# Attention and two MLPs on one core: the float64 sign kept by a parametric ReLU, the rounding given to the engine that is free, another order of the first sixteen steps, reloads in place

## The chip, the cores and the metric

The kernel runs on one core of a Trainium2 chip. The metric is the device time of one execution in microseconds, of which the median over several executions is compared. An execution that is recorded by the hardware profiler gives the trace; its span runs from its first to its last instruction.

## The reference

Attention over q, k, v (4 batches, 8 heads, 576 rows, 64 wide) is the sum of a coarse part, softmax over rows averaged by four, repeated four times, and a local part, softmax over the rows at a distance under four. Its output, 2304 rows of 512, goes through two layers of the same form:

```python
def _moe_ref(x, w_in, w_out):          # layer 1; _moe2_ref is the same with its own weights
    h = x @ w_in                       # 2304x512 @ 512x2048
    r = np.maximum(h, 0.0)
    g = r * r
    return (g @ w_out).astype(np.float32)   # 2304x2048 @ 2048x512
```

q, k and v are float32. The weights w_in and w_out are float64.

## The kernel before

**Tiles and steps.** The 2304 rows are cut into nine tiles of 256 rows, the 2048 hidden columns into eight pieces p of 256. A step (n, p) multiplies tile n with piece p of w_in (`mm_h`, L883: 24 matmuls, two halves of 12), takes ReLU and square on ScalarE (L895, L897), splits g into a high part (L907, ScalarE) and a low part (L934, VectorE), and multiplies with piece p of w_out (`mm_y`, L967: 24 matmuls). Every operand is split in two because TensorE takes fp32r: `xH`, `xL` of a tile (`split_x`, L390 and L858), high and low halves of a weight. The product y of a step stands in TensorE's order after the h of the next step. n from 0 to 8 is layer 1, n from 9 to 17 layer 2, where w_out is multiplied in seven products instead of eight (`mm_y2`, L950). The first sixteen steps belong to tiles 0 and 1 together; `LEAD` says how far tile 0 is ahead. Both tiles need each weight only once it has been converted.

**Weights of layer 1** (`convert1`, sixteen pieces of 1 MB float64). A piece lands in a buffer `s` as pairs of 32-bit words. ScalarE scales the upper words to a float32 in `gp` (1024 columns) or `ga` (two of 512) (L693), ScalarE shifts the lower words (L695), VectorE puts the sign bit of the upper word into the lower one (L697), VectorE joins the two (L702), ScalarE rounds the result to the high part (`evac`, L390), VectorE or GpSimd subtracts it to get the low part (L713). There are two such sets of buffers, so two pieces are in work at a time. `convert2` does the same for layer 2 in 32 halves during layer 1 (L739, L741, L743, L747) and stores the joined float32 in DRAM (`ws`). `reload` fetches it back when tile 8 has used a piece for the last time: into a buffer `ld`, of which there are two, then high part (L390) and low part (L829). `quarters` prepares the seven products' sums of w_out.

**Attention.** Rows of a batch are taken in five groups of 116. Per batch, `load_qk` transposes q and k in five chunks (L450, evacuated by L390, pooled by four on VectorE at L457), `heads_of` does the coarse part, `group` the local one: scores (L586), maximum, exponential, sum, division (L619, on VectorE or GpSimd), transposition (L623), product with the values (L641, values loaded by `values`, L556), addition into the tile `xr` (L653). Tile 0 needs groups 0 to 2 of batch 0, tile 1 needs groups 2 to 4.

**What sets the order.** All instructions of an engine run in the order in which the program issues them. That order is worked out by `Order`, a list scheduler with a cost for every operation: each thread has a priority, a number from the tables `CP, CD, GP, UP, QP, VP, HP`, and asks for an engine and a time. An operation that may run on several engines gives a list, and the engine is taken on which it would end first. `dvp` and `pool` stand for VectorE and GpSimd with a common port in that planner, `dve` and `fast` for VectorE without it. Until the first step TensorE is given small products without use (`fill`, L1121) in every gap of the plan. All DMAs are issued by SyncE, in order; each waits for the DMA eight before it.

## Time and profile before

| | us |
|---|---|
| three executions, median | 926.19 (924.8 to 1109.7) |
| the profiled execution | 928.45 |
| its span | 926.6 |
| TensorE busy with matmuls | 895.9 (97%) |
| VectorE busy | 533.5 (58%) |
| ScalarE busy | 525.2 (57%) |
| GpSimd busy | 70.4 (8%) |

A share over the span says little here, since the first 92 us (attention of batch 0, weights on their way) and the rest are different stages. One reads first where TensorE is idle or slow, and then what it waits for there.

### The profile page before, as it was taken

Reading aid. Unit: us, or ns where it says so; the run is one execution under the profiler, and the core shown is the slowest. Engines: PE = TensorE matmul, PEld = TensorE weight load, DVE = VectorE, ACT = ScalarE, POOL = GpSimd, SP = SyncE. Lnnn points to the kernel's source line nnn. Section 1 sums busy time; section 2 is a strip of 40 time slices with the busy share of each in tenths; the row PEclk is TensorE's granted clock in tenths of the full one; section 3 lists DMA queues with packets and bytes.
Section 4 is the critical chain, followed back from the end, with each engine's and each line's share of the span. In section 5 each row is a group of like instructions: output and inputs, shape, how many; then the busy total and the mean of one; then the engine's idle time right before and its main releaser. Section 6 shows DMA issues by size and latency. Waiting matters only on the chain.

```text
span 926.6 us, 20891 instructions
## 1 busy us (share of the span) xinstructions
PE 895.9 (97%) x8712; PEld 860.9 (93%) x8712; DVE 533.5 (58%) x1072; ACT 525.2 (57%) x1029; POOL 70.4 (8%) x72
## 2 busy tenths in 40 slices
PE   8967999999999999999999999999999999999996
PEld 5566999999989999999999999999999999999996
DVE  5898875375685656554412466646556464545454
ACT  4787884466467566664535665455555554545443
POOL 4102210020030100000100001000000000000000
PEclk9978999999999999999999999999999999999999
DMA  9997931135255665753203441101010010100000
GB/s 173 248 247 187 229 100 36 48 109 125 52 163 170 185 196 183 238 182 102 93 1 138 137 159 48 46 1 46 2 46 24 24 47 1 47 1 24 1 24 23
DMA packets 91998, 90.48 MB, mean 98 GB/s; under 512 B 62208, under 2 KB 67840, under 8 KB 91904
## 3 DMA queue, kind: packets, MB, share of 16 engines
q1 hardware_dynamic: 91904, 89.15, 33.9%
q8 instruction: 68, 1.11, 0.5%
q14 instruction: 26, 0.21, 0.1%
HBM read 70.25 MB, written 18.87 MB: 96 GB/s over the span
## 4 chain that ended last, share of the span: by engine, by line
PE 85%; DVE 5%; DMA 4%; ACT 3%; SPq 2%; issue 1%; ACTq 0%; DVEq 0%
PE h L883 40%; PE y L967 19%; PE at L950 12%; PE y L950 4%; PE at L967 2%; DMA s<-in_moe_w_out_dram 1%; PE at L450 1%; DVE S L930 1%; DMA ld<-in_v_dram 1%; SPq L437 1%; DVE ld L1072 1%; PE at L641 1%; PE at L586 1%; PE at L516 1%; PE at L476 1%
## 5 line engine op out<-in xcount | busy, mean ns | idle before, releaser
L883 PE MATMUL h<-xH,w 128*128 128x256 f32 x2304 | 318.7, 281 | 0.0
L883 PEld LDWEIGHTS h<-xH,w 128*128 128x128 f32 x2304 | 289.0, 189 | 2.4 <-issue 1.6
L895 ACT ACTIVATE h<-h 128x512 f32<-128x512 f32 x144 | 83.9, 583 | 195.6 <-PE h L883 195.5
L967 PE MATMUL y<-g,w 128*128 128x256 f32 x1536 | 193.1, 280 | 0.2 <-ACT g L907 0.2
L967 PEld LDWEIGHTS y<-g,w 128*128 128x128 f32 x1536 | 182.2, 189 | 3.2 <-issue 1.2
L883 PE MATMUL h<-xL,w 128*128 128x256 f32 x1152 | 180.2, 279 | 0.0
L934 DVE TENSOR_TENSOR g<-h,g 128x512 fp32r<-128x512 f32 x144 | 98.6, 684 | 106.2 <-ACT g L907 105.8
L883 PEld LDWEIGHTS h<-xL,w 128*128 128x128 f32 x1152 | 154.7, 189 | 0.0
L930 DVE TENSOR_TENSOR S<-h,S 128x128 f32<-128x128 f32 x144 | 41.9, 291 | 154.8 <-ACT g L907 150.5
L913 ACT CAST SH<-S 128x512 fp32r<-128x512 f32 x72 | 44.7, 621 | 93.2 <-DVE S L930 91.0
L897 ACT ACTIVATE h<-h 128x512 f32<-128x512 f32 x144 | 84.2, 585 | 3.1
L907 ACT CAST g<-h 128x512 fp32r<-128x512 f32 x144 | 84.8, 589 | 1.5
L939 DVE TENSOR_TENSOR gSL<-S,SH 128x512 fp32r<-128x512 f32 x72 | 51.1, 709 | 9.9 <-ACT SH L913 1.5
L858 POOL TENSOR_TENSOR xL<-xr,xH 128x512 fp32r<-128x512 f32 x12 | 18.0, 1504 | 408.2 <-ACT xH L390 408.2
L950 PE MATMUL at<-w,SH 128*128 128x256 f32 x224 | 45.0, 282 | 1.4 <-ACT SH L913 1.4
L930 DVE TENSOR_TENSOR S<-S,h 128x128 f32<-128x128 f32 x144 | 41.2, 286 | 5.0
L950 PEld LDWEIGHTS at<-w,SH 128*128 128x128 f32 x224 | 34.0, 188 | 2.3 <-ACT SH L913 2.2
L950 PE MATMUL at<-w,g 128*128 128x256 f32 x240 | 34.6, 279 | 0.4 <-DVE g L934 0.4
L950 PE MATMUL at<-w,gSL 128*128 128x256 f32 x112 | 32.1, 287 | 1.9 <-DVE gSL L939 1.9
L950 PEld LDWEIGHTS at<-w,g 128*128 128x128 f32 x240 | 30.8, 188 | 0.6 <-DVE g L934 0.6
L950 PE MATMUL y<-w,g 128*128 128x256 f32 x192 | 27.6, 279 | 0.0
L457 DVE TENSOR_REDUCE qkd<-at 128x256 f32<-128x1024 f32 (+1 forms) x19 | 20.7, 1106 | 9.3 <-ACT qkT L390 9.1
(252 smaller groups left out, 1238.0 us busy)
## 6 DMA issues: line engine op xcount, KB each, us to landing
ld<-ws SPq DMA_DIRECT2D x24, 512.0 KB, 3.2
s<-in_moe_w_in_dram SPq DMA_DIRECT2D x32, 256.0 KB, 3.7
s<-in_moe_w_out_dram SPq DMA_DIRECT2D x16, 512.0 KB, 10.9
ws<-ga SPq DMA_DIRECT2D x32, 256.0 KB, 2.4
ld<-in_moe_w_in_dram SPq DMA_DIRECT2D x11, 512.0 KB
ld<-in_moe_w_out_dram SPq DMA_DIRECT2D x11, 512.0 KB, 4.7
xr<-ys SPq DMA_DIRECT2D x9, 512.0 KB, 3.7
vw<-in_v_dram SPq DMA_DIRECT2D x68, 64.0 KB, 3.0
```

The costliest lines, as they stand in the source:

```text
L457: nc.vector.tensor_reduce(out=qkd[:, :, :, 32 * c:32 * c + n // 4], in_=got.rearrange("p z m (g r) -> p z m g r", r=4), op=ALU.add, axis=AX.X,
L858: engine().tensor_tensor(out=xL[n % NXL][:, ks], in0=xr[i][:, ks], in1=xH[n % NXL][:, ks].bitcast(F32), op=ALU.subtract)
L883: nc.tensor.matmul(out=o, lhsT=wt[p, 0][:, 1084:1340][:, fs] if w is wL and kk == 0 and p in ODD else w[:, kk, fs], rhs=x[:, kk], start=(i ...
L895: nc.scalar.activation(out=h, in_=h, func=AF.Relu)
L897: nc.scalar.activation(out=h, in_=h, func=AF.Square)
L907: nc.scalar.copy(g_of(i, 0), h)
L913: nc.scalar.copy(late2["SH"], late2["S"])
L930: nc.vector.tensor_tensor(out=dst, in0=a, in1=b, op=op)
L934: nc.vector.tensor_tensor(out=g_of(i, 1), in0=h, in1=g_of(i, 0).bitcast(F32), op=ALU.subtract)
L939: nc.vector.tensor_tensor(out=late2["SL"], in0=late2["S"], in1=late2["SH"].bitcast(F32), op=ALU.subtract)
L950: nc.tensor.matmul(out=seven(n, m - 1), lhsT=lhsT, rhs=quarter(p, w, low), start=p == 0 and x == 0 and m not in (2, 3, 6), stop=p == NP - ...
L967: nc.tensor.matmul(out=yb[e // 2][:, (e % 2) * 256:(e % 2) * 256 + 256], lhsT=w[:, fi, e * 128:e * 128 + 128], rhs=g[:, fi * 256:fi * 256 ...
```

## The change

It has five parts. (1) L693 and L739 scale the upper word with a parametric ReLU (slope 2^32 for negative values) in place of a plain copy, so that the sign survives the shift; L697 and L743, which carried it over on VectorE, are gone (16 instructions of 1024 columns, 32 of 512). (2) The rounding to the high part in `convert1` goes to ScalarE or VectorE, whichever the planner finds free first; the cost of `fast` has no port in it. (3) The first sixteen steps follow the string `TURNS`, digit by digit the tile: three of tile 0, two of tile 1, and so on; before they were three of tile 0, then tile 1 and tile 0 in turn until tile 0 had its eight. (4) The numbers that set priorities are others, and three are new. (5) `reload` loads straight into the place of the low part, rounds from there and subtracts in place, and takes no buffer `ld`; `quarters` runs as one thread in place of two.

```diff
-LEAD = 2
+TURNS = "0001101011000111"
-CP, CD, GP, UP = -0.47, 0.09, -1.99, -1.02
-QP, VP, HP = -0.59, 0.34, -0.14
+CP, CD, GP, UP = -0.705, 0.436, -1.416, -0.816
+QP, VP, HP = -0.053, 0.649, 0.159
+CK, H1, G1 = 0.243, 0.689, -0.199
...
         for g, c, n in parts:
             yield act(n)
-            nc.scalar.activation(out=g, in_=wf[:, c:c + n], func=AF.Copy, scale=2.0 ** -112)
+            nc.scalar.activation(out=g, in_=wf[:, c:c + n], func=AF.Prelu, scale=2.0 ** -112, alpha=2.0 ** 32)
         yield act(1024)
         nc.scalar.activation(out=wl, in_=wl, func=AF.Copy, scale=2.0 ** -29 - 2.0 ** -49, bias=-0.5)
-        yield dvp(1024)
-        nc.vector.scalar_tensor_tensor(
-            out=w32[:, :, 0], in0=w32[:, :, 1], scalar=-2 ** 31, in1=w32[:, :, 0], op0=ALU.bitwise_and, op1=ALU.bitwise_or
-        )
...
         for g, c, n in parts:
-            yield act(n)
-            evac(hi[:, c:c + n], g)
+            yield [act(n), fast(n)]
+            if o.eng == "ACT":
+                evac(hi[:, c:c + n], g)
+            else:
+                nc.vector.tensor_copy(hi[:, c:c + n], g)
...
-        n = yield from f_ld.take()
-        t = ld[n].bitcast(F32)
-        yield dma(128 * 4096)
-        nc.sync.dma_start(out=t, in_=wscr[p][kind])
         hi = weight(p, kind, 0, 2).rearrange("p k f -> p (k f)")
-        yield act(1024)
-        evac(hi, t)
-        for lo, c, n1 in pieces(p, kind, 1, 2, 0, 1024):
+        some = pieces(p, kind, 1, 2, 0, 1024)
+        for lo, c, n1 in some:
+            yield dma(128 * 4 * n1, 4096 if n1 == 1024 else 2048)
+            nc.sync.dma_start(out=lo.bitcast(F32), in_=wscr[p][kind][:, c:c + n1])
+        for lo, c, n1 in some:
+            yield act(n1)
+            evac(hi[:, c:c + n1], lo.bitcast(F32))
+        for lo, c, n1 in some:
             tt = yield either(n1)
-            engine().tensor_tensor(out=lo, in0=t[:, c:c + n1], in1=hi[:, c:c + n1].bitcast(F32), op=ALU.subtract)
-        f_ld.put(n, tt)
+            engine().tensor_tensor(out=lo, in0=lo.bitcast(F32), in1=hi[:, c:c + n1].bitcast(F32), op=ALU.subtract)
...
-    steps = []
-    for p in range(NP + LEAD):
-        steps += [(0, p)] * (p < NP) + [(1, p - LEAD)] * (p >= LEAD)
+    steps = [(int(n), TURNS[:i].count(n)) for i, n in enumerate(TURNS)]
...
-    o.lane(2, [(98, quarters(0)), (98, quarters(1))])
+    o.lane(1, [(98, quarters())])
```

Since the planner works on these numbers, most rows of the first stage stand elsewhere; line numbers of the changed kernel are two or three off. Three places follow. `s_88`, `s_89`, `s_90` are the float64 pieces of w_in for p = 0, 1, 2; `s_65`, `s_68`, `s_71` those of w_out; `w_629`, `w_715`, `w_663` (before) and `w_499`, `w_680`, `w_576` (after) the converted p = 0 and 1 of w_in and p = 0 of w_out; `e_84` holds the scores of groups 2 to 4 and `e_95` their values.

VectorE before, up to the division of group 4 (`e_84<-e_84,nmb_76`), for which TensorE waits at 58.8 us:

```order
L702 SCALAR_TENSOR_TENSOR gp<-gp,s_89 128x1024
L613 TENSOR_REDUCE nmb_76<-e_84 128x8
L615 TENSOR_SCALAR nmb_76<-nmb_76 128x8
L697 SCALAR_TENSOR_TENSOR s_68<-s_68 128x1024
L713 TENSOR_TENSOR w_715<-gp,w_715 128x1024
L653 TENSOR_TENSOR xr_104<-y,outd 128x4x58
L702 SCALAR_TENSOR_TENSOR ga_86<-ga_86,s_68 128x512
L653 TENSOR_TENSOR xr_104<-y,outd 128x4x58
L702 SCALAR_TENSOR_TENSOR ga_87<-ga_87,s_68 128x512
L617 RECIPROCAL nmb_76<-nmb_76 128x8
L619 TENSOR_TENSOR e_84<-e_84,nmb_76 128x2x4x64
L697 SCALAR_TENSOR_TENSOR s_90<-s_90 128x1024
```

VectorE after, the twelve rows up to the same division:

```order
L655 TENSOR_TENSOR xr_103<-at_118,outd 128x4x24
L701 SCALAR_TENSOR_TENSOR gp<-gp,s_89 128x1024
L655 TENSOR_TENSOR xr_104<-at_118,outd 128x4x34
L711 CAST w_680<-gp 128x1024
L655 TENSOR_TENSOR xr_104<-at_118,outd 128x4x58
L607 TENSOR_TENSOR e_84<-at_117,nmb_76 128x2x4x64
L615 TENSOR_REDUCE nmb_76<-e_84 128x8
L617 TENSOR_SCALAR nmb_76<-nmb_76 128x8
L619 RECIPROCAL nmb_76<-nmb_76 128x8
L857 TENSOR_TENSOR xL_101<-xr_103,xH_99 128x512
L701 SCALAR_TENSOR_TENSOR ga_86<-ga_86,s_68 128x512
L621 TENSOR_TENSOR e_84<-e_84,nmb_76 128x2x4x64
```

Ahead of the division the sign instructions (L697) and the subtractions for `w_663` and `w_715` are gone from VectorE, a cast to `w_680` has come in, and the two additions of group 3 into `xr_104` stand behind it.

TensorE before, around the first step (`w_629`):

```order
L641 MATMUL y<-e_84,e_95 64x58 x16
L883 MATMUL h_120<-xH_99,w_629 128x256 x8
L883 MATMUL h_120<-xL_101,w_629 128x256 x4
L623 MATMUL at_118<-ident,e_84 128x128 x4
L883 MATMUL h_120<-xH_99,w_629 128x256 x8
L883 MATMUL h_120<-xL_101,w_629 128x256 x4
L883 MATMUL h_121<-xH_99,w_715 128x256 x8
L883 MATMUL h_121<-xL_101,w_715 128x256 x4
L641 MATMUL at_117<-e_84,e_95 64x58 x4
L641 MATMUL at_117<-e_84,e_95 64x54 x4
L641 MATMUL at_117<-e_84,e_95 64x58 x4
L641 MATMUL at_117<-e_84,e_95 64x54 x4
```

TensorE after, around the same step (`w_499`):

```order
L880 MATMUL h_120<-xH_99,w_499 128x256 x8
L880 MATMUL h_120<-xL_101,w_499 128x256 x4
L643 MATMUL at_118<-e_84,e_95 64x58 x16
L625 MATMUL at_117<-ident,e_84 128x128 x4
L880 MATMUL h_120<-xH_99,w_499 128x256 x8
L880 MATMUL h_120<-xL_101,w_499 128x256 x4
L880 MATMUL h_121<-xH_99,w_680 128x256 x8
L880 MATMUL h_121<-xL_101,w_680 128x256 x4
L643 MATMUL at_118<-e_84,e_95 64x58 x4
L643 MATMUL at_118<-e_84,e_95 64x54 x4
L643 MATMUL at_118<-e_84,e_95 64x58 x4
L643 MATMUL at_118<-e_84,e_95 64x54 x4
```

Group 3's product with the values, which stood ahead of the first step, stands between its two halves.

SyncE before, the loads that follow the values of groups 0 and 1 (`vw_108`, `vw_109`):

```order
L678 DMA s_88<-in_moe_w_in_dram 64x2x256 x4
L683 DMA s_65<-in_moe_w_out_dram 128x512 x2
L678 DMA s_89<-in_moe_w_in_dram 64x2x256 x4
L683 DMA s_68<-in_moe_w_out_dram 128x512 x2
L556 DMA e_95<-in_v_dram 64x4x64 x5
L678 DMA s_90<-in_moe_w_in_dram 64x2x256 x4
L556 DMA e_95<-in_v_dram 64x4x64 x4
L683 DMA s_71<-in_moe_w_out_dram 128x512 x2
L556 DMA e_95<-in_v_dram 64x4x64 x2
L678 DMA s_91<-in_moe_w_in_dram 64x2x256 x4
L556 DMA e_95<-in_v_dram 64x4x64
```

SyncE after, the loads that follow the values of group 0:

```order
L680 DMA s_88<-in_moe_w_in_dram 64x2x256 x4
L685 DMA s_65<-in_moe_w_out_dram 128x512 x2
L558 DMA vw_109<-in_v_dram 64x4x64 x4
L680 DMA s_89<-in_moe_w_in_dram 64x2x256 x4
L685 DMA s_68<-in_moe_w_out_dram 128x512 x2
L558 DMA e_95<-in_v_dram 64x4x64 x4
L680 DMA s_90<-in_moe_w_in_dram 64x2x256 x4
L558 DMA e_95<-in_v_dram 64x4x64
L685 DMA s_71<-in_moe_w_out_dram 128x512 x2
L558 DMA e_95<-in_v_dram 64x4x64 x3
L680 DMA s_91<-in_moe_w_in_dram 64x2x256 x4
L558 DMA e_95<-in_v_dram 64x4x64 x4
```

The weights for p = 0 go ahead of group 1's values; of the four loads for group 3 (the second four of `e_95`) three stand behind `s_71`, and group 4's four behind `s_91`.

## Rows read from the trace of the kernel before

**Rows 1.** The page: busy time of each engine, share of the span, instructions.

```profile
PE 895.9 (97%) x8712; PEld 860.9 (93%) x8712; DVE 533.5 (58%) x1072; ACT 525.2 (57%) x1029; POOL 70.4 (8%) x72
```

**Rows 2.** Stages: busy us (instructions) of each engine, granted clock, DMA share, GB/s.

```profile
25.00:49.80 24.80, 21.52 (x317) 13.00 (x316) 21.25 (x45) 19.35 (x42) 1.23 (x2) 0.98 0.98 244
49.80:91.70 41.90, 28.69 (x258) 27.14 (x255) 36.53 (x48) 32.22 (x45) 5.71 (x5) 0.81 0.93 217
91.70:538.00 446.30, 445.46 (x4703) 432.54 (x4700) 247.82 (x445) 264.72 (x530) 38.66 (x32) 1.00 0.45 133
538.00:594.00 56.00, 53.31 (x455) 52.06 (x454) 37.72 (x80) 33.75 (x63) 3.69 (x2) 1.00 0.22 79
594.00:917.00 323.00, 322.37 (x2751) 320.90 (x2749) 171.11 (x423) 163.43 (x325) 9.93 (x6) 1.00 0.06 21
```

**Rows 3.** Waits of TensorE: line waited for, us in total, times, longest.

```profile
PE at L450 <- DVE qkd L457: 6.5, 1, 6.5
...
PE at L623 <- ACT w L390: 6.2, 1, 6.2
...
PE at L950 <- DVE gSL L939: 1.9, 6, 0.8
```

**Rows 4.** Timeline of TensorE: start, us, instruction, idle time before it.

```profile
48.52 1.38 PE L641 MATMUL y<-e,e 64*64 64x58 f32 x30 [1.76 <-DMA e<-in_v_dram]
...
49.83 2.08 PE L883 MATMUL h<-xH,w 128*128 128x256 f32 x8
...
58.82 1.09 PE L623 MATMUL at<-ident,e 128*128 128x128 f32 x4 [6.22 <-ACT w L390]
...
82.67 1.97 PE L450 MATMUL at<-ident,e 128*128 128x128 f32 x8 [6.51 <-DVE qkd L457]
...
91.68 1.19 PE L883 MATMUL h<-xH,w 128*128 128x256 f32 x8
```

**Rows 5.** Timeline of VectorE, four of its instructions.

```profile
23.36 1.07 DVE L492 TENSOR_SCALAR nm<-nm 72x4 f32<-72x4 f32 x1
...
27.69 0.15 DVE L492 TENSOR_SCALAR nm<-nm 72x4 f32<-72x4 f32 x1
...
57.98 0.69 DVE L619 TENSOR_TENSOR e<-e,nmb 128x512 f32<-128x512 f32 x1
...
81.40 2.35 DVE L457 TENSOR_REDUCE qkd<-at 128x256 f32<-128x1024 f32 x2
```

**Rows 6.** Timeline of GpSimd, one instruction.

```profile
23.37 1.03 POOL L619 TENSOR_TENSOR pb<-pb,nmb 128x512 f32<-128x512 f32 x1
```

**Rows 7.** Groups of instructions: line, shapes, count, busy us, mean ns, idle before.

```profile
L697 DVE SCALAR_TENSOR_TENSOR s<-s 128x1024 int32<-128x1024 int32 x16 | 19.6, 1222 | 6.6 <-ACT s L695 6.4
...
L713 DVE TENSOR_TENSOR w<-gp,w 128x1024 fp32r<-128x1024 f32 x5 | 6.1, 1222 | 1.2 <-ACT w L390 1.2
...
L390 ACT ACTIVATE w<-gp 128x1024 fp32r<-128x1024 f32 x8 | 8.5, 1058 | 5.8 <-DVE gp L702 5.8
...
L713 POOL TENSOR_TENSOR w<-gp,w 128x1024 fp32r<-128x1024 f32 x1 | 2.6, 2606 | 25.7 <-ACT w L390 25.7
...
L858 POOL TENSOR_TENSOR xL<-xr,xH 128x512 fp32r<-128x512 f32 x12 | 18.0, 1504 | 408.2 <-ACT xH L390 408.2
```

**Rows 8.** Timeline of SyncE, which issues the DMAs.

```profile
43.84 2.58 SPq L556 DMA_DIRECT2D e<-in_v_dram  x4
...
87.34 0.35 SPq L683 DMA_DIRECT2D s<-in_moe_w_out_dram  x1
```

**Rows 9.** The chain that ended last: start, us, what.

```profile
437.18 2.72 PE y L967 x24
...
647.14 2.83 PE h L883 x24
```

**Rows 10.** Two stretches of the ramp, columns as in rows 2.

```profile
48.00:62.00 14.00, 7.26 (x57) 6.91 (x58) 13.78 (x20) 9.72 (x15) 0.00 (x0) 0.65 1.05 277
...
82.70:87.00 4.30, 4.30 (x23) 4.30 (x24) 3.01 (x4) 2.60 (x4) 4.22 (x5) 0.57 0.39 91
```

More of the change, by code (lines that the diff above doesn't have):

```diff
@@ L738, in convert2 @@
         yield act(512)
-        nc.scalar.activation(out=g, in_=wf, func=AF.Copy, scale=2.0 ** -112)
+        nc.scalar.activation(out=g, in_=wf, func=AF.Prelu, scale=2.0 ** -112, alpha=2.0 ** 32)
         yield act(512)
         nc.scalar.activation(out=wl, in_=wl, func=AF.Copy, scale=2.0 ** -29 - 2.0 ** -49, bias=-0.5)
-        yield dvp(512)
-        nc.vector.scalar_tensor_tensor(
-            out=w32[:, :, 0], in0=w32[:, :, 1], scalar=-2 ** 31, in1=w32[:, :, 0], op0=ALU.bitwise_and, op1=ALU.bitwise_or
-        )
         tt = yield dvp(512)
@@ L780, in make_room, with quarters @@
         ev["room"] = 0.0
-    def quarters(p0):
+    def quarters():
         yield lambda: ev.get("room")
-        for p in range(p0, NP, 2):
+        for p in range(NP):
             n = yield from f_ld.take()
@@ L976, in ybs @@
     def ybs(n):
-        return [pair[1][:, i] for i in range(2)] if n == 1 and LEAD < NP else yb
+        return [pair[1][:, i] for i in range(2)] if n == 1 else yb
     def products():
@@ L982, in y @@
             yield o.at("gh", i)
-            if p == 0 and n > (LEAD < NP) and n < NT:
-                yield o.at("left", n - 1 if n != 2 or LEAD == NP else 0)
+            if p == 0 and n > 1 and n < NT:
+                yield o.at("left", n - 1 if n != 2 else 0)
             if seq[n][0] == 2:
@@ L1025, in products @@
                 yield from f_at.give_up([2])
-            if LEAD < NP and (n, p) == (1, 0):
+            if (n, p) == (1, 0):
                 yield from f_at.give_up([1])
@@ L1077, in leave @@
             ev["left", n] = tt
-            if n == 1 and LEAD < NP:
+            if n == 1:
                 f_at.back(1, tt)
@@ L1092, in attention_two_mlp_kernel @@
     for b in range(B):
-        t = b * S / TN - 2
+        t = b * S / TN - 2 + (b == 1) * H1
         heads += [(t + QP, load_qk(b, c)) for c in range(5)]
@@ L1096, in attention_two_mlp_kernel @@
         heads += [(t + HP, heads_of(b, hp)) for hp in range(4)]
-        vees += [((b * S + GQ * i) / TN + UP, values(b, i)) for i in range(NG)]
-        groups += [((b * S + GQ * i) / TN + GP, group(b, i)) for i in range(NG)]
-    first_w = [(CP + CD * p, convert1(p, kind)) for p in range(NP) for kind in range(2)]
+        vees += [((b * S + GQ * i) / TN + UP + (b == 1) * H1, values(b, i)) for i in range(NG)]
+        groups += [((b * S + GQ * i) / TN + GP + (b == 1) * G1, group(b, i)) for i in range(NG)]
+    first_w = [(CP + CD * p + CK * kind, convert1(p, kind)) for p in range(NP) for kind in range(2)]
     second_w = [(99, convert2(p, kind, half)) for p in range(NP) for kind in range(2) for half in range(2)]
```

## The prediction

> **What bounds the kernel now.** I read the busy line first [rows 1]: TensorE is busy 97% of the span, so an instruction taken from another engine counts only where TensorE waits for it. The stages [rows 2] say where that is. From 91.7 to 538 us TensorE is busy 445.46 of 446.30, and from 594 to 917 it is 322.37 of 323; VectorE has work for 247.82 of the 446. In these two stretches a shorter VectorE gives nothing. What is left is the ramp, 49.8 to 91.7, with 28.69 busy of 41.9 and a granted clock of 0.81, and the change of layer, 538 to 594, with 2.7 idle. Before 49.8 the DMA share is 0.98, and TensorE is fed with small products; nothing in the change makes bytes fewer.
>
> The list of waits [rows 3] gives 12.7 of the 13.2 idle microseconds of the ramp to two: 6.5 at L450 for VectorE's pooling L457, and 6.2 at L623. The list puts the second down to ScalarE's rounding L390, but TensorE's timeline has its end at 58.8 [rows 4] and VectorE's division of group 4, L619, begins at 57.98 and takes 0.69 [rows 5]: TensorE waits for that. Between 48 and 62 VectorE is busy 13.78 of 14 [rows 10], so it is VectorE's queue that bounds this stretch, not data.
>
> A second loss is not idle time. Around both waits the granted clock is low: 0.65 over 48 to 62, 0.57 over 82.7 to 87 [rows 10], and 12 matmuls at 59.56 take 2.06 + 1.05 us where at 91.68 the first eight take 1.19 instead of 2.06 or 2.08 [rows 4]. I reckon the sound work of the ramp: three h and three y of 24 matmuls at 2.72 [rows 9] are 16.3; the transpositions of five chunks, from 1.97 for eight at the low clock, about 1.0 for eight at the high one, are 4.9; the rest of the attention about 2.2. That is 23.4 of 28.7 busy, so 5.3 are lost to the clock at its level of 1.2 GHz. Together 13.2 + 5.3 = 18.5 us of the ramp are lost, about 9.6 at the first wait and 8.9 at the second.
>
> **The change, part by part.** *The sign on ScalarE.* ScalarE's scaling is one instruction as before; the trace has no parametric ReLU, and I take the same time for it, between 0 and 10% more (another function of the same engine). VectorE loses 16 x 1.22 = 19.6 us [rows 7] and about as much in layer 2's halves. Of this only what stands ahead of the two waits counts. In the order four of L697 stood ahead of group 4's division (for `s_88`, `s_65`, `s_89`, `s_68`): 4 x 1.22 = 4.9. For the same division the new order also drops 2048 columns of subtraction, now on GpSimd (2 x 1.22, the time of a 1024-column instruction of VectorE: 2.4), half of one split of x (0.7), a join of 512 columns (0.7) and two additions of group 3 (0.8): 9.5 off.
>
> *The rounding on VectorE* puts back three casts, 2560 columns. No row shows this cast on VectorE. ScalarE takes 1.058 per 1024 and VectorE 1.222 for an instruction with one stream in [rows 7]; I take the lower, 2.6 us, since a cast reads one operand only, and keep as ends 3.1 and 0, since an instruction cannot take less than nothing. Net 6.9: the division ends at about 51.8 in place of 58.7. The Trainium skill, "VectorE: DVE Perf Modes" (section on the perf-mode tier table), has a float32 copy from SBUF at twice the rate of a two-operand instruction; by it the casts would be some 1.6 us (an estimate), and the division would end one microsecond earlier; no row here shows it.
>
> *What is late next at the first wait.* Not VectorE but the values of group 3. Before, they were issued from 43.84 on [rows 8] and landed at 48.5, ahead of the first step, and TensorE waited 1.76 us for them [rows 4]. In the new order three of their four loads stand behind the 1 MB of `s_71`, which at 277 GB/s [rows 10] takes 3.8 us: 52.3. TensorE meets them between the two halves of the first step. The first half may start at 48 to 50 and runs at the low clock; then 52.3, the product with the values 0.7, the transposition, and the second half begins at about 54 where it was 59.56. Gain 5.6. A little of the 9.6 stays: some 1 us idle and 2 to 3 of clock; the values of group 4, behind `s_91`, land at about 57, with 2 halves of h (5 us at that clock) to run until then. I put the gain of this part at 6.
>
> *The second wait.* At 76.2 TensorE had run out of buffers for transposed chunks, since VectorE pools them late: L457 at 81.40 is two instructions, 2.35 [rows 5], behind sign instructions and joins. In the new order only two of the eight-transposition groups stand ahead of the first step of tile 1 (five before, a y or a piece of it between), and the rest lie among full steps later, where TensorE has always a matmul to go on with. So this wait goes with its 1.9 of clock loss: up to 8.4. I take 7.5, since chunk 1's q and k are issued later (after `s_92` as before, but after one more wait of SyncE) and may leave 1. Three groups of eight are owed and are paid at about 1.0 (half of 1.97) each after the ramp; that is a shift of work, no gain, and isn't counted. Sum of the ramp: 6 + 7.5 = 13.5 of 18.5 lost.
>
> *The order of steps.* Tile 0's pieces 3 to 7 were the steps in places 4, 6, 8, 10, 12, counted from 0; now 5, 7, 10, 11, 12. A step is 48 matmuls, 5.4 us, so pieces 3 to 6 are due one or two steps later, but all steps 13.5 us earlier; the last is due at about 78 + 9 x 5.4 = 127. A piece pair is 2.1 MB, 9.7 us at 217 GB/s [rows 2], against 10.9 us for two steps. SyncE issued a piece at 87.34 after a stand behind the buffers of the chunks [rows 8]; five of the sixteen pieces come after that, at 4.8 us each: 111, and with conversion (scaling, shift, join, rounding and subtraction, each about 1.1) 117. Margin of 10: cost 0, with 5 as the upper end if a stand like that of 87 comes again.
>
> *GpSimd.* It is used far more in the ramp: two subtractions of 1024 columns at 2.61, four of 512 at half of that, three splits of x at 1.50 [rows 7], a division at 1.03 [rows 6]: some 16 us of instructions where it had 5.71 [rows 2]. One place of the trace shows what this does to VectorE: at 23.36 an instruction of four columns, elsewhere 0.15, takes 1.07 [rows 5], while GpSimd's division runs from 23.37 for 1.03 [rows 6]. So it loses up to 0.9 per microsecond of GpSimd. I take 2 us of the path for it (bounds 0 and 8): of the 16, half meet VectorE in a sensitive instruction, and a third of that lies ahead of something TensorE waits for. The Trainium skill, "SBUF — State Buffer" (section "Who interferes with whom"), speaks against this part: copies and casts are among what takes the port that VectorE shares with GpSimd, and the second to issue stands still for the whole of the other's instruction; rows 5 and 6 agree with the standing still. The planner gives the cast no port.
>
> *Reload in place* starts no earlier in principle (the place is free when tile 8 has read it), but no longer waits for one of two buffers. Of 2.7 us of idle in the change of layer, 1.9 are waits for VectorE's L939 [rows 3], which the new order relieves only in part: gain 1, bounds 2.7 and -2 (two more DMAs per piece in SyncE's queue). `quarters` as one thread lies in layer 1, where nothing waits: 0.
>
> **The sum** against the profiled execution, 928.45: 13.5 - 2 + 1 = 12.5, so 915.9. That execution is 2.3 above the median, 926.19, and the same amount off the median gives 913.7; I say 913.5.
>
> **Rivals.** (a) *The port decides.* If VectorE stands for 0.9 of each of GpSimd's 16 us in the ramp, 14 us, and a half of that lies ahead of a wait, the loss is 7 instead of 2, and casts take 1.2 rather than 1.06 per 1024: 919 to 920. For it: VectorE is full there and the planner doesn't see it. Against it: the reductions and the small instructions, most of its list, run alone in many places.
> (b) *The ramp loses nearly nothing.* The first wait shrinks, and with no long idle stretch the clock does not fall: all 18.5 and 2.7 come back: 905. For it: the granted clock is 1.00 wherever TensorE is kept busy [rows 2]. Against it: the values of groups 3 and 4 land late.
> (c) *DMA bounds the ramp.* Bytes are unchanged and the DMA share is 0.93 to 1.05 there; VectorE's relief then turns into waits for landing, and 1 or 2 us are left of the gain: 924 to 926. Against it: 6.5 of the 12.7 come from VectorE's pooling alone.
> (d) *Slower: TensorE's pace.* The chain shows 24 matmuls at 2.72 us at 437 and at 2.83 at 647 [rows 9], both at a granted clock of 1.00. The slower pace is 4% and in the trace holds for stretches, beginning after short waits (594 on follows the waits of the change of layer). If the new order, which has more short waits in the first steps, puts 91.7 to 538 on that pace, 446 x 0.04 = 18 us are added: 926 - 12.7 + 18 = 931. It decides from 318 us of slow pace on (12.7 / 0.04). Against it: the waits of the ramp did not start it before.
>
> **Chances.** Forecast 0.5, (a) 0.2, (b) 0.2, (c) 0.05, (d) 0.05. The range must keep 8 in 10: from 903 ((b), with something below it left out) to 923 (above (a) and the bounds of casts, GpSimd and weights), leaving (c), (d) and the tails. About 2% is what a measurement of this kernel can tell from no change: faster by that is under 907.7, which is most of (b) and a little of the forecast's low end, 0.21; slower is over 944.7, for which (d) alone does not suffice: 0.02; within 2%: 0.77.
>
> **What would show it.** In the changed profile: the first h at 48 to 50; TensorE's wait between the halves of the first step on a DMA into e (values of group 3), not on VectorE; the second half at 53 to 55; the first step of tile 1 at 75 to 78, with no wait of 6 us at the transposition of chunks; the granted clock of 48 to 62 above 0.75; casts (L711) at 0.6 to 1.2 us per 1024; idle in the change of layer under 2.7. A second half after 57 with the division on VectorE or GpSimd as its releaser speaks for (a); a step of 24 matmuls at 2.83 before 538 for (d); waits on weights w after 90 would say that the reckoning of the later pieces failed. The number is most at risk in the late values, and in 24 matmuls whose pace I don't understand.

## The result, and the profile after

The changed kernel's median is 917.32 us (915.75 to 918.36, four executions) beside 926.19 for the kernel before (924.8 to 930.53, three executions; a fourth, disturbed one of 1109.7 is left out): the recorded ratio is 0.9889 (95% interval 0.9858 to 0.9919). Measured again on another occasion, in the experiments below, it was 914.24 (912.87 to 918.27, five executions) beside 925.25, a ratio of 0.9888 (0.9871 to 0.9904). So the change takes off 1.1%, some 10 us: 8.9 by the medians of the first occasion, 11.0 by those of the second. The forecast was 913.5.

The page of the profiled execution (918.11 us, span 916.3), where VectorE has 29 us less work than in [rows 1]:

```profile
PE 894.6 (98%) x8712; PEld 856.6 (93%) x8712; DVE 504.4 (55%) x1025; ACT 515.4 (56%) x1015; POOL 81.5 (9%) x84
```

The stages, columns as in [rows 2]:

```profile
25.00:49.80 24.80, 21.61 (x267) 13.22 (x266) 15.71 (x37) 16.75 (x36) 3.70 (x4) 0.72 0.97 245
49.80:91.70 41.90, 36.43 (x363) 33.44 (x363) 35.59 (x50) 31.53 (x46) 14.07 (x9) 0.96 0.98 207
91.70:538.00 446.30, 445.98 (x4704) 432.81 (x4703) 231.43 (x415) 267.32 (x533) 43.31 (x39) 1.00 0.47 140
538.00:594.00 56.00, 53.55 (x448) 52.70 (x448) 30.30 (x73) 26.98 (x54) 1.29 (x1) 0.97 0.07 25
```

In the ramp TensorE has 36.43 busy of 41.9 where it had 28.69, and the granted clock is 0.96 where it was 0.81. But before the ramp, from 25 to 49.8, the clock is 0.72 where it was 0.98, and the change of layer has 0.97. The waits of TensorE that answer to [rows 3], with 12.7 us in two:

```profile
PE h L880 <- DVE xL L857: 2.6, 1, 2.6
PE at L579 <- DVE qkd L459: 2.2, 3, 1.6
PE at L947 <- ACT SH L910: 1.9, 1, 1.9
```

TensorE's timeline around the first step and at tile 1's first step, beside [rows 4]:

```profile
52.91 1.16 PE L880 MATMUL h<-xH,w 128*128 128x256 f32 x8
...
56.93 0.50 PE L880 MATMUL h<-xL,w 128*128 128x256 f32 x2 [2.63 <-DVE xL L857]
...
59.02 2.06 PE L880 MATMUL h<-xH,w 128*128 128x256 f32 x8
...
82.23 1.19 PE L880 MATMUL h<-xH,w 128*128 128x256 f32 x8
```

The first h is 3.1 us later than before (49.83), its second half as late (59.02 beside 59.56), and tile 1's step comes 9.4 earlier (91.68 before). In the second profile of the same kernel (label `again`, 912.87 us) the same four rows are:

```profile
47.51 1.18 PE L880 MATMUL h<-xH,w 128*128 128x256 f32 x8
...
51.57 0.50 PE L880 MATMUL h<-xL,w 128*128 128x256 f32 x2 [2.65 <-DVE xL L857]
...
53.79 1.89 PE L880 MATMUL h<-xH,w 128*128 128x256 f32 x8
...
76.94 1.19 PE L880 MATMUL h<-xH,w 128*128 128x256 f32 x8
```

All four are 5.2 to 5.4 us earlier. Why one kernel has two ramps is the matter of experiments 10 and 11. To compare kernels further down I take the start of ScalarE's ReLU of a step (one instruction a step, 144 of them, so that as many steps are done at step i in each) and subtract that of the kernel before. Up to step 24, and in some kernels up to step 40, the rows still hold attention that one kernel does earlier than another. Step 72 is the first of layer 2:

```
us against the profile of before, at step  3     8    24    40    72    80   143
changed kernel (first profile)           -9.3  -7.4  -6.5  -6.9  -6.9  -6.1 -10.1
again (the same kernel)                 -14.6 -12.8 -11.8 -11.9 -11.9 -11.7 -15.3
sign_only                               +22.4 +22.7 +26.8 +18.1 +23.9 +23.9 +21.0
loads_together                           -7.4 -10.1  -0.8  -1.4  -1.4  -1.4  -2.3
sign_back                                +2.4  +3.4  +5.5  +4.3  +4.3  +3.5  +3.5
turns_old                               -12.7  -1.0  +3.4  -2.0  -2.0  -2.9  -5.8
round_act                               -13.4 -13.1  -5.6  -6.4  -6.4  -5.7  -9.6
round_port                              -13.3  -7.5  -6.5  -7.3  -7.3  -6.6  -7.4
no_pool                                  -8.1  -5.9  -5.2  -5.5  -5.5  -3.8  -6.4
fill5                                   -12.3 -10.3  -9.3  -9.6  -9.6  -8.9 -11.7
late_3                                  -11.3 -10.5  -9.6  -9.9  -9.9  -9.4 -12.3
reload_only                              -0.6  -0.6  -0.9  -0.9  -0.9  -1.8  -5.7
kick3                                   -13.7 -11.9 -10.9 -11.3 -11.3 -10.5 -10.9
```

Between step 40 and step 72 nothing moves, except in `sign_only`. What comes behind step 80 is put down to no part of the change (fourth experiment).

### The profile page after: what moved, and what is told of

Its sections match the earlier page's. It is cut to its first block, busy times and chain, and to the rows that moved or that the text cites. A ratio compares the mean times of both kernels' runs of the same rounds, so it can differ in the third digit from the quotient of the medians.

```text
span 916.3 us, 20841 instructions
## 1 busy us (share of the span) xinstructions
PE 894.6 (98%) x8712; PEld 856.6 (93%) x8712; DVE 504.4 (55%) x1025; ACT 515.4 (56%) x1015; POOL 81.5 (9%) x84
## 4 chain that ended last, share of the span: by engine, by line
PE 79%; DVE 8%; DMA 5%; ACT 4%; SPq 2%; issue 2%; ACTq 0%
PE h L880 37%; PE y L964 19%; PE at L947 11%; PE y L947 4%; DMA s<-in_moe_w_out_dram 2%; PE at L964 2%; DVE S L927 2%; DVE ld L1069 2%; DMA s<-in_moe_w_in_dram 1%; DVE xL L857 1%; DMA vw<-in_v_dram 1%; DVE gSL L936 1%; PE at L452 1%; SPq L439 1%; PE at L643 1%
## 5 line engine op out<-in xcount | busy, mean ns | idle before, releaser
L880 PE MATMUL h<-xH,w 128*128 128x256 f32 x2304 | 315.4, 280 | 0.0
L880 PEld LDWEIGHTS h<-xL,w 128*128 128x128 f32 x1152 | 152.7, 188 | 2.8 <-DVE xL L857 2.8
L927 DVE TENSOR_TENSOR S<-h,S 128x128 f32<-128x128 f32 x144 | 41.9, 291 | 153.4 <-ACT g L904 145.4
L857 POOL TENSOR_TENSOR xL<-xr,xH 128x512 fp32r<-128x512 f32 x16 | 21.5, 1346 | 463.5 <-ACT xH L392 463.2
L947 PE MATMUL at<-w,gSL 128*128 128x256 f32 x112 | 32.1, 287 | 1.9 <-DVE gSL L936 1.8
L1118 PE MATMUL h<-ident 128*128 128x512 bf16 x89 | 25.8, 428 | 1.6 <-DVE ident L1126 1.6
```

The source lines that it names most:

```text
L857: engine().tensor_tensor(out=xL[n % NXL][:, ks], in0=xr[i][:, ks], in1=xH[n % NXL][:, ks].bitcast(F32), op=ALU.subtract)
L880: nc.tensor.matmul(out=o, lhsT=wt[p, 0][:, 1084:1340][:, fs] if w is wL and kk == 0 and p in ODD else w[:, kk, fs], rhs=x[:, kk], start=(i ...
L927: nc.vector.tensor_tensor(out=dst, in0=a, in1=b, op=op)
L947: nc.tensor.matmul(out=seven(n, m - 1), lhsT=lhsT, rhs=quarter(p, w, low), start=p == 0 and x == 0 and m not in (2, 3, 6), stop=p == NP - ...
L1118: nc.tensor.matmul(out=hb[1], lhsT=ident16, rhs=ident16.unsqueeze(1).to_broadcast([128, 4, 128]), start=True, stop=True)
```

## The experiments

The theory: VectorE's relief empties the ramp of its two waits, and that is the gain. The rivals: the order (numbers, turns) makes it without the relief; or the reload; or it is eaten by the port that VectorE and GpSimd share, at which one stands still while the other works (called a lock below). All ratios are to the kernel before in the same session.

**1. The sign alone** (`sign_only`): the kernel before with only

```diff
-func=AF.Copy, scale=2.0 ** -112
+func=AF.Prelu, scale=2.0 ** -112, alpha=2.0 ** 32
```

and without L697 and L743.

> The kernel before with the sign kept by the parametric ReLU and nothing else (old numbers, old turns, rounding on ScalarE, reload through its buffers). Theory 1, VectorE's relief is what frees the ramp: 5 us or more under the kernel before, 919 to 922, and both long waits of TensorE in the ramp (6.5 and 6.2) fall under 3. Theory 2, the gain comes from the other numbers and the order of the first sixteen steps: within 2 us of the kernel before, with a wait of 5 or more still standing between 50 and 92 us.

Measured: 948.2 us, ratio 1.0249 (1.0225 to 1.0273), slower by 23 us; neither theory had that. SyncE's and TensorE's timelines:

```profile
94.60 0.60 SPq L556 DMA_DIRECT2D e<-in_v_dram  x1
```

```profile
103.35 1.09 PE L623 MATMUL at<-ident,pb 128*128 128x128 f32 x4 [4.25 <-DVE pb L605]
...
111.76 1.09 PE L623 MATMUL at<-ident,pb 128*128 128x128 f32 x4 [6.28 <-DVE pb L619]
112.50 2.06 PE L875 MATMUL h<-xH,w 128*128 128x256 f32 x8
```

One of group 4's four loads of values is issued at 94.6, behind q, k and five pieces of weights. Without it tile 1 is not complete; its first step begins at 112.50, where it was at 91.68. TensorE multiplies with those values at 104.4, behind the first of the two waits shown, which are for VectorE's work on other scores (`pb`). The planner issues whatever can start first; that with cheaper conversions a weight could always start ahead of that load is my reading of its rule, and no row shows it.

**2. The same with the loads in one block** (`loads_together`):

```diff
-        for c, _, _, w0 in blocks_of(i):
-            for j in range(2):
-                tt = yield "SP", 0.29, 1.2
+        tt = yield "SP", 4 * 0.29, 4 * 1.2
+        for c, _, _, w0 in blocks_of(i):
+            for j in range(2):
```

> The kernel before with the sign on ScalarE alone, and the four loads of a group's values issued as one block. Theory 1: what made that kernel slow (948) is one load of group 4's values behind q, k and four pieces of weights, issued at 94.6 us, without which tile 1 could not begin; with it in place 916 to 923. Theory 2: with the old numbers the planner's order is bad in more places: above 930.

Measured: 925.18 us, ratio 1.0003 (0.9992 to 1.0014). With the loads in one block the 23 us are gone, but the relief by itself is worth nothing; the time lies between the two theories. The block alone, without the relief, was not run. Its timeline of TensorE, and three stages:

```profile
63.97 5.49 PE L959 MATMUL y<-g,w 128*128 128x256 f32 x24 [5.72 <-ACT g L899]
```

```profile
49.80:91.70 41.90, 34.29 (x321) 32.24 (x321) 28.20 (x41) 32.87 (x49) 0.74 (x1) 0.92 0.98 227
91.70:165.00 73.30, 72.82 (x775) 68.98 (x774) 42.23 (x73) 50.98 (x103) 6.20 (x4) 1.00 0.47 110
165.00:200.00 35.00, 31.94 (x395) 30.49 (x394) 20.10 (x36) 17.27 (x29) 2.68 (x3) 0.95 0.34 87
```

VectorE has 28.20 of 41.9 left to do in the ramp (36.53 before), yet TensorE waits 5.7 us there for ScalarE's high part of the square of the first step, and 3.1 between 165 and 200, at the transposition of a chunk of q and k, where the clock falls too. The ramp is 10.1 us ahead at step 8 and 0.8 at step 24; what the waits don't explain of this I take for attention that was put off, which no row here shows.

**3. All but the sign** (`sign_back`): the changed kernel with L697 and L743 put back and AF.Copy for Prelu.

> The changed kernel with the sign carried over on VectorE again (L697 and L743 of before), new numbers and turns, rounding on either engine, reload in place. Theory 1, the gain needs VectorE's relief: 922 to 928. Theory 2, the order makes it and the relief is hidden by the landing of values: 915 to 919.

Measured: 926.31, ratio 1.0015 (1.0000 to 1.0030): no gain either. The ramp as a stage, and TensorE's timeline at its longest wait:

```profile
49.80:91.70 41.90, 27.30 (x258) 24.86 (x258) 37.51 (x55) 28.82 (x39) 9.80 (x7) 0.80 0.98 226
```

```profile
86.82 3.64 PE L972 MATMUL y<-g,w 128*128 128x256 f32 x16 [6.55 <-ACT g L912]
```

VectorE is at 37.51 of 41.9, and TensorE waits 6.6 for the high part of a square on ScalarE, which stands behind conversions that wait for VectorE (1.7, 0.5 and 0.3 us between 76 and 82). Experiments 2 and 3 together: neither half has any gain, both have 1.1%. Within the order, the new numbers and the new turns are told apart by one run only (experiment 9); the new turns with the old numbers were not run.

**4. The reload alone** (`reload_only`): the kernel before with the new `reload` and `quarters`; TensorE's order is that of before.

> The kernel before with reload in place and quarters as one thread and nothing else; TensorE's order is that of the kernel before row for row. Theory 1: the change of layer loses 2.7 us before and gains at most 1, so 0 to 1 us under the kernel before. Theory 2: the 3.2 us by which the changed kernel gains between the square of step 72 and that of step 143 come from the reload: 3 us under the kernel before, with TensorE's pace in layer 2 better than before. If that pace is chance of a run, layer 2 differs by 0 to 3 us either way from profile to profile and no part of the change makes it.

Measured: 925.95, ratio 1.0008 (0.9989 to 1.0027), twelve executions against seventeen. Its profile gains 0.9 at the change of layer (steps 72 to 80, idle 2.4 instead of 2.7), and then 3.9 to the end. But that execution was its fastest (922.53; the others reach 929.23), and the table shows the same 3.6 to 4.0 behind step 80 in two profiles with the new reload (the changed kernel's) and 0.0 to 0.8 in two others that also have it (`sign_back`, `round_port`): it isn't the reload. By the starts of the steps it is a pace: a step of layer 2 takes 5.10 us or 5.30 (in the shorter pace two steps at the turn of each tile take up to 1 us more, so that eight steps take 41.9 us or 42.4), and the kernel before has the longer one from step 82 to 95 and from 114 to the end in its profile, `reload_only` nowhere, `round_port` from 114 on. The change of layer:

```profile
538.00:594.00 56.00, 53.55 (x463) 52.71 (x462) 34.36 (x74) 30.95 (x60) 3.40 (x2) 1.00 0.15 48
```

**5. Small products against the longer pace** (`kick3`):

```diff
-KICK = {(n, 1) for n in (10, 12, 14)}
+KICK = {(n, 1) for n in (10, 12, 14)} | {(n, 3) for n in range(10, 18)}
```

> The changed kernel with one more small product without use ahead of step p = 3 of the tiles 10 to 17 (it goes into a half of h that the next product overwrites). In the profiles a step of layer 2 takes 5.10 us or 5.30; the longer one begins at p = 2 of tile 10 or 14, by chance of the run, and ends at the small product of tile 12. If that product ends it, no run keeps it for more than a step: 912 to 916, and the runs spread by less than 2 us. If it has nothing to do with it: as the changed kernel, 915 to 919, spread by 3 to 6.

Measured: 918.84, ratio 0.9928 (0.9911 to 0.9946), slower than the changed kernel. In its profile, by the starts of the steps, each small product that came in the longer pace ended it, at (11, 3), (14, 1), (15, 3) and (17, 3). But of the seven that came in the shorter pace four began the longer one, at (10, 3), (13, 3), (14, 3) and (16, 3). In the kernels without the added products the longer pace begins at the same place in the tiles 10, 12 and 14 (before, at steps 82 and 114), so only (13, 3) and (16, 3) are new places. So theory 1 has half of it right, and the edit is of no use.

**6 and 7. The rounding.** `round_act` has `yield act(n)` and ScalarE alone; `round_port` gives the cast the port:

```diff
-            yield [act(n), fast(n)]
+            yield [act(n), ("DVP", fast(n)[1])]
```

> The changed kernel with the rounding of convert1 always on ScalarE. Theory 1, the casts on VectorE save ScalarE's time at a price in locks with GpSimd (1.6 us instead of some 0.8 per 1024 columns in the trace): the two balance, 915 to 919, VectorE's first waits alike. Theory 2, ScalarE becomes the bound of the ramp without them: 921 or more, with TensorE waiting for a converted weight before the step of tile 1.

> The changed kernel with the cast's cost in the planner as one that takes the port which VectorE shares with GpSimd, so that the planner puts no GpSimd work beside a cast. Theory 1, the locks cost 2 to 4 us of the ramp: 913 to 916. Theory 2, they lie beside other waits (landing values): 916 to 919, as the changed kernel, with the casts at 0.8 us per 1024 columns all the same.

Measured: 918.54, ratio 0.9937 (0.9914 to 0.9960), and 917.54, ratio 0.9920 (0.9896 to 0.9943). By their times theory 1 of the first and theory 2 of the second hold. The rounding on VectorE gives some 4 of the 10 us (by ratios of two sessions), and a plan that keeps casts away from GpSimd gives nothing: of its casts up to 92 us two of 512 columns still meet GpSimd (1.41 and 0.84 us), the two of 1024 take 0.68. But the planner's whole order is another there, so the price of the locks alone isn't measured. `round_port` has its first step early, and then meets what stands next (TensorE's timeline, and a stage):

```profile
47.83 1.18 PE L880 MATMUL h<-xH,w 128*128 128x256 f32 x8
...
53.03 1.56 PE L643 MATMUL at<-e,e 64*64 64x58 f32 x30 [1.76 <-DMA e<-in_v_dram]
...
59.14 0.63 PE L625 MATMUL at<-ident,e 128*128 128x128 f32 x4 [1.75 <-DVE e L621]
```

```profile
92.00:110.00 18.00, 16.07 (x160) 15.04 (x160) 12.05 (x20) 12.72 (x26) 4.27 (x4) 0.95 1.02 201
```

TensorE waits 1.8 for the values of group 3, 1.8 for a division on VectorE, and 1.9 between 92 and 110 on batch 1's attention: 13.3 us ahead at step 3, 7.3 at step 40.

**8. GpSimd off** (`no_pool`): between the last chunk of batch 0 and tile 1's first step every choice between VectorE and GpSimd goes to VectorE.

```diff
-        return [dvp(cols), pool(cols)]
+        return [dvp(cols), pool(cols)] if ev.get(("h", 1, 0)) is not None or ev.get(("qkT", 0, 4)) is None else [dvp(cols)]
```

> The changed kernel with every choice between VectorE and GpSimd, from the last chunk of q and k of batch 0 until tile 1's first step, made for VectorE. Theory 1, GpSimd's relief is worth more than its locks: VectorE has some 7 us more work in the ramp, the second half of the first step later by 3 or more, 917 to 921. Theory 2, locks cost as much as the relief gives (a cast of 1024 columns at 1.6 us beside GpSimd, 0.8 alone): 913 to 917.

Measured: 920.16, ratio 0.9921 (0.9892 to 0.9950). Theory 1 by its time. By the ratios GpSimd is worth some 3 us here, locks and all; but the interval overlaps with the changed kernel's (0.9871 to 0.9904). TensorE's timeline at its longest wait, where VectorE's division comes late:

```profile
54.46 1.12 PE L625 MATMUL at<-ident,e 128*128 128x128 f32 x4 [6.71 <-DVE e L621]
```

The casts as groups of instructions, first of this kernel, then of `again`:

```profile
L711 DVE CAST w<-ga 128x512 fp32r<-128x512 f32 x10 | 4.1, 418 | 0.1
...
L711 DVE CAST w<-gp 128x1024 fp32r<-128x1024 f32 x3 | 2.1, 685 | 0.0
```

```profile
L711 DVE CAST w<-gp 128x1024 fp32r<-128x1024 f32 x7 | 7.6, 1083 | 0.1
...
L711 DVE CAST w<-ga 128x512 fp32r<-128x512 f32 x8 | 4.8, 613 | 0.1
```

A cast of 1024 columns takes 685 ns alone. The 1083 of `again` is a mean of two kinds: three of the seven meet no instruction of GpSimd and take 681 to 695 ns, four meet one and take 1.08 to 1.65 us.

**9. The old turns** (`turns_old`): the changed kernel with

```diff
-TURNS = "0001101011000111"
+TURNS = "0001010101010111"
```

> The changed kernel with the first sixteen steps in the old order (three of tile 0, then tile 1 and tile 0 in turn) and all else new. Theory 1, that order is no part of the gain, since the first four steps are the same and the weights land in time: within 2 us of the changed kernel, 913 to 917. Theory 2, tile 0's later steps must be put off for the weights: TensorE waits for a converted weight between 90 and 130 us, 918 or more.

Measured: 923.62, ratio 0.9980 (0.9965 to 0.9995). Theory 2, with 9 of the 10 us (the numbers were chosen together with the new turns). ScalarE's timeline at the piece p = 5 of w_in, TensorE's at the step that needs it, and the stage:

```profile
106.30 0.66 ACT L696 ACTIVATE ga<-s 128x512 f32<-128x512 f32 x1 [3.03 <-DMA s<-in_moe_w_in_dram]
```

```profile
106.45 2.99 PE L964 MATMUL y<-g,w 128*128 128x256 f32 x24
...
116.09 2.08 PE L880 MATMUL h<-xH,w 128*128 128x256 f32 x8
```

```profile
91.70:130.00 38.30, 31.59 (x292) 28.88 (x291) 29.29 (x43) 28.39 (x60) 8.57 (x7) 0.96 0.80 196
```

The piece has landed at 106.3 and is converted at 116; the ninth step needs it. From 109 to 116 TensorE has only attention of batch 1, with a wait of 0.6 to 1.1 at each product, and the clock falls: the step at 116.09 takes 2.08 for eight products that take 1.19 at the clock's higher level. With the new turns that piece is needed by the eleventh step; in `again` it lands at 104.4, hardly earlier.

**10 and 11. The two ramps of the changed kernel.** ScalarE's timeline in the first profile and in `again`:

```profile
29.98 1.12 ACT L696 ACTIVATE gp<-s 128x1024 f32<-128x1024 f32 x1 [1.67 <-DMA s<-in_moe_w_in_dram]
```

```profile
28.59 1.11 ACT L696 ACTIVATE gp<-s 128x1024 f32<-128x1024 f32 x1
```

In the first, ScalarE stands 1.67 us at L696 for the landing of the first piece of weights, with the heads' work behind it; TensorE waits 1.62 for that at L518 (its timeline, then the stages that follow):

```profile
31.68 1.23 PE L518 MATMUL at<-hd,vd 72*64 72x144 f32 x8 [1.62 <-ACT hd L392]
```

```profile
30.00:30.50 0.50, 0.06 (x1) 0.00 (x0) 0.00 (x0) 0.50 (x1) 0.00 (x0) 0.79 1.03 196
30.50:31.00 0.50, 0.00 (x0) 0.00 (x0) 0.00 (x0) 0.50 (x2) 0.00 (x0) 0.50 1.28 217
...
30.00:34.00 4.00, 2.38 (x16) 1.49 (x17) 0.00 (x0) 3.54 (x9) 0.00 (x0) 0.54 1.05 207
34.00:38.00 4.00, 4.00 (x23) 2.54 (x21) 2.37 (x6) 2.18 (x6) 0.00 (x0) 0.50 0.94 255
38.00:42.00 4.00, 4.00 (x47) 2.28 (x46) 3.34 (x7) 3.55 (x6) 0.00 (x0) 0.50 1.09 264
42.00:46.00 4.00, 4.00 (x26) 2.16 (x24) 2.54 (x6) 2.19 (x4) 0.00 (x0) 0.76 0.78 178
```

The clock is near its lower level, 1.2 GHz, from 30.5 to some 44 us, and even the small products without use hold up what follows. In `again` there is no such wait and the clock is 1.00. What the low clock costs can be read from the same products in both. TensorE's timeline in the first profile, then in `again`:

```profile
46.35 0.69 PE L643 MATMUL at<-pb,vw 64*64 64x58 f32 x32
```

```profile
30.37 0.71 PE L518 MATMUL at<-hd,vd 72*64 72x144 f32 x8
...
39.81 0.69 PE L643 MATMUL at<-pb,vw 64*64 64x58 f32 x32
```

From L518 to that product, without idle time in either, the first profile takes 14.7 us (31.68 to 46.35) and `again` 9.4 (30.37 to 39.81). So 1.3 us come from the wait and 5.2 from the clock; of these 6.5, 5.4 are left at the first h. `fill5` puts five small products ahead of L518, and nothing else changes on any engine; `late_3` tells the planner that the piece lands 3 us later.

> The changed kernel with five more small products without use on TensorE ahead of the first product of the heads (L518); every other engine's order is that of the changed kernel row for row. In one profile of the changed kernel TensorE waited 1.6 us there, since ScalarE stood 1.7 at L696 for the landing of the first weights, the granted clock went to 0.50 from 31 to 43 us, and all that follows was 5 us later than in the other profile, which had no such wait. Theory 1, the idle time at that place costs it by the clock: the clock stays at 1.00 there, the step of tile 1 begins at 77 to 78 in the profile, the median is 912.5 to 914.5. Theory 2, the late landing itself costs it, whatever the clock: as the changed kernel, 914 to 918, with the ramp late wherever ScalarE stands at L696.

> The changed kernel with 3 us more in the planner for the landing of the first piece of weights, so that ScalarE's scaling of it (L696) stands behind the work of the heads that TensorE waits for; the planner's order is another from there on. Theory 1: no wait of ScalarE for a landing ahead of the heads, clock 1.00 until 45 us, median 912 to 915 unless the other order has a wait of its own. Theory 2, that place doesn't matter: 914 to 918.

Measured: 914.62, ratio 0.9882 (0.9861 to 0.9903), and 914.49, ratio 0.9880 (0.9859 to 0.9902). Neither is to be told from the changed kernel (0.9888 and 0.9889). In the profile of `fill5` the clock is 1.00 there, but ScalarE did not stand at L696 in that execution, so it does not decide between its theories. In that of `late_3` ScalarE does not stand at L696 and the clock is 1.00 until 46 us, as theory 1 has it, but the other order has waits of its own (3.2 us for a load of values, 2.6 for a division on GpSimd), and the clock is 0.50 to 0.61 from 46 to 58. That the low clock makes all that follows 5 us later is seen in the two profiles of one kernel. What lowers it is not shown: it falls between 30 and 31 us, when the wait (30.06 to 31.68) has only begun, and the idle 0.95 us shortly before, ahead of L508, stands in both profiles. Nor is it shown that mending it lowers the median, or which of the two ramps is the usual one.

**12. The changed kernel again** (`again`), used throughout. It came in at 914.24, just under its range, with a ramp of 11.9 in place of 7.

> The changed kernel unchanged, beside the next three on the same chip. 7 us under the kernel before from the ramp (what the profiles show at step 24 and after), and the rest by the pace of layer 2: 915 to 919 where the kernel before has 924 to 926.

## Why the prediction was right, and where not

**The stage and the size.** The forecast placed the gain in the ramp: 13.5, less 2 for GpSimd. At step 40 it is 6.9 in the first profile and 11.9 in the second. Of what it named as signs, the second profile has the second half of the first step (53 to 55 forecast, 53.79), tile 1's step (75 to 78, 76.94) and the clock of 48 to 62 (above 0.75, 0.88); its first h is half a microsecond early (48 to 50, 47.51). Up to the second half of the first step it gains 5.8, where 6 was put down. The first profile is 2.9 to 4.2 us later than these ranges, by a step that I didn't have: the loads of the first weights moved ahead, and with them ScalarE's scaling, in front of the heads; I looked for what was queued behind on SyncE and VectorE, not on ScalarE. So the nearness of the medians has some luck in it: which of the two ramps an execution has, and the pace of layer 2, are no terms of the sum.

**The wait that takes over.** Named as the values of group 3, between the halves of the first step; it was VectorE's low part of x (L857, 2.6 in both profiles), inside the first half, behind a join and a cast that GpSimd stretched. VectorE's timeline in `again`, then GpSimd's:

```profile
44.90 1.63 DVE L701 SCALAR_TENSOR_TENSOR gp<-gp,s 128x1024 int32<-128x1024 int32 x1
...
46.66 1.57 DVE L711 CAST w<-gp 128x1024 fp32r<-128x1024 f32 x1
...
50.88 0.64 DVE L857 TENSOR_TENSOR xL<-xr,xH 128x512 fp32r<-128x512 f32 x1
```

```profile
44.40 1.04 POOL L621 TENSOR_TENSOR e<-e,nmb 128x512 f32<-128x512 f32 x1 [1.06 <-DVE nmb L619]
45.72 1.96 POOL L857 TENSOR_TENSOR xL<-xr,xH 128x512 fp32r<-128x512 f32 x1 [0.27 <-ACT xH L392]
```

The join takes 1.63 where `no_pool` has 1.22, the cast 1.57 where it has 0.69: 1.3 us in VectorE's order ahead of L857, of the 2 that were put down for GpSimd. With the casts' port in the plan the values of group 3 do become the wait, at 53.03, close to the forecast of 52.3.

**The casts.** The three ahead of the division were put at 2.6 us, with ends of 0 and 3.1. They took 0.68 + 1.41 + 1.57 = 3.66 in `again`, outside those ends, and 0.68 + 0.42 + 1.57 = 2.67 in the first profile: a cast is cheaper than the 1.06 per 1024 taken, and dearer where it meets GpSimd, so the term came near in one profile for the wrong reason. The upper end came from 1222 [rows 7], read as the time of an instruction with one stream; L697 joins two words of `s` and L713 reads two tiles, so both have two. The division ends at 52.7 in `again`, beside 51.8 forecast. The Trainium skill, "VectorE: DVE Perf Modes" (perf-mode tier table), has a float32 copy at twice the rate of a two-operand instruction: 685 ns beside 1222 [rows 7], 1.8 times, nearly agrees. The Trainium skill, "SBUF — State Buffer" (Who interferes with whom), has casts among what locks the port that VectorE shares with GpSimd, so that the second to issue stands still: 1.08 to 1.65 us beside 0.68 to 0.70 agrees in kind. But rival (a), that this decides, is not borne out by experiments 7 and 8: with most of the locks gone there is no more gain, and with GpSimd's work moved to VectorE there is less. GpSimd's work in the ramp was 14.1 and 11.0 us in the two profiles, not 16.

**The sign on ScalarE** was put at the time of the plain copy, and that holds. The scaling before, then in `again`:

```profile
L693 ACT ACTIVATE gp<-s 128x1024 f32<-128x1024 f32 x8 | 9.2, 1147 | 2.5 <-DVE w L713 2.5
```

```profile
L696 ACT ACTIVATE gp<-s 128x1024 f32<-128x1024 f32 x9 | 10.4, 1157 | 4.6 <-DMA e<-in_k_dram 2.3 <-DMA s<-in_moe_w_out_dram 0.8 <-DVE w L715 0.8
```

**The second wait** was to go, for 7.5: of the 6.5 for the pooling of chunks 1.6 remain in the ramp (L579; 2.2 in the whole trace), and the steps from the second half of the first to tile 1's first took 23.2 us in both profiles where they took 32.1, so 8.9. 2.5 of that are paid back by step 6 for the chunks moved behind, where about 3 was forecast, so some 6.4 are gained where 7.5 was put down; GpSimd's locks are in that already.

**The order of steps** was put at no cost, which holds: from 90 to 250 us TensorE waits 0.3 us in both profiles, and never for a weight. But that was the wrong question. Experiment 9 shows that the old one would have given back 9 of the 10 us. I reckoned when pieces land, found a margin of 10 for the last one and did not look at p = 5 under the old turns; and the last piece, reckoned to land by 111, was issued only at 116.3 in `again`. And nothing in the prediction says that the relief without the new numbers is worth nothing, as experiment 2 shows.

**Reload in place**, +1: 0.9 in the one profile in which it stands alone, no difference in the medians; in the changed kernel the change of layer lost 0.75 in the first profile and 0.2 in the second, where steps 72 to 80 are compared.

**The other rivals.** (b) fell short: 5.5 of idle (3.9 in `again`) and a clock of 0.96 remain. Its ground, a clock of 1.00 wherever TensorE is kept busy, was against [rows 10] already (busy 4.30 of 4.30, clock 0.57), and from 34 to 42 us in the first profile it fails again. (c) isn't seen: TensorE's waits in the ramp are for VectorE and ScalarE. (d) did not come: the steps of layer 1 without attention keep 5.44. The 3.2 us between the profile of before and the first one after, from step 72 to the end, are the pace, which the kernel before had against it in its profiled execution. One profile of that kernel doesn't show how often it does.

## What to carry to other kernels

A relief that empties one queue pays only if the order behind it moves too: here the same relief of VectorE was worth 1.1% with a new order (and the rounding on either engine), nothing with the old one, and minus 2.5% when one small load fell behind. So cost an edit together with what is needed next, one step further than the wait it removes. When an in-order engine gets an instruction that waits for a landing, look at whose work stands behind it. And take two profiles of a kernel before a difference of 5 us is explained.

## What the runs showed of the hardware that was not expected

In one of two profiles of the same kernel TensorE's clock fell between 30 and 31 us, at the start of a wait of 1.6 us, and stayed at its lower level until some 44 us, also while TensorE was kept busy (34 to 42, 8.00 of 8.00 busy, clock 0.50). It cost 5.2 us on products that took 9.4 at the higher level. A step of layer 2, 45 matmuls, has two paces at a granted clock of 1.00, 5.10 us and 5.30; which one holds differs from execution to execution of one kernel, and both turns are seen at a small product of 128 columns, the one to the longer pace also without it. In layer 1 only one pace (5.44 for 48 matmuls) was seen. What sets the pace stays open.
